# Decoding of the weights: the conversion from bfloat16 to float16 on GpSimd in place of ScalarE

## The chip, the core and the metric

The kernel runs on one core of a Trainium2 chip (trn2). The core has five engines, each with an instruction queue of its own: TensorE (PE, matmuls; PEld is its weight load), VectorE (DVE), ScalarE (ACT), GpSimd (POOL) and SyncE (SP, which here only issues DMAs). An engine works through its queue in order, and a semaphore holds an instruction back until what it needs has been done elsewhere. The metric is the device time of one execution in microseconds (us), lower is better.

## What is computed

Random-feature attention over 8 batches of 8 heads, and a feed-forward block on its output:

```python
def _attn_ref(q, k, v, omega):
    m, D = omega.shape
    scale = 1.0 / np.sqrt(np.sqrt(D))
    q_s, k_s = (q * scale, k * scale)
    def phi(x):
        proj = np.einsum('bhsd,md->bhsm', x, omega)
        sq = np.sum(x * x, axis=-1, keepdims=True) / 2.0
        h = proj - sq
        h = h - np.max(h, axis=-1, keepdims=True)
        return np.exp(h) / np.sqrt(m)
    q_p, k_p = (phi(q_s), phi(k_s))
    kv = np.einsum('bhsm,bhsd->bhmd', k_p, v)
    z = np.sum(k_p, axis=2)
    num = np.einsum('bhsm,bhmd->bhsd', q_p, kv)
    den = np.einsum('bhsm,bhm->bhs', q_p, z)[..., None] + 1e-06
    return num / den

def _moe_ref(x, w_in, w_out):      # x: 4608 x 512, d_ff 2048
    h = x @ w_in
    g = h - np.tanh(h)
    return g @ w_out
```

All inputs are float32. Batch 8, 8 heads, 576 positions, head size 64, 128 features.

## The kernel before

**Tiling.** The 4608 tokens go through in ten chunks (two of 256, eight of 512). The feed-forward block splits d_ff = 2048 into 16 slices of 128, called f0 to ff in the order strings. For each chunk and slice TensorE makes `h` (line 563, 12 matmuls, as each float32 product is made of three: high by high, high by low, low by high part), ScalarE takes the tanh, VectorE subtracts, ScalarE rounds the result to a high part, VectorE makes the low part, and TensorE then adds the slice to the output sums `po` (lines 589 to 591, 12 matmuls).

**The order.** Nothing is left to a scheduler. Two strings list every step: ORDER covers the first chunks, where batches 0 and 1 of the attention, the decoding of the weights and the first pass over the 16 slices are mixed; LATER covers the rest. A token `d4.b.0` reads: unit d (decoder) of slice 4, step b, argument 0. Each engine's queue holds its instructions in the order of the tokens, whatever the engine.

**The decoder.** The weights of all 16 slices come in once, at the start, and each slice is decoded in five steps before its first use:

- `is` (line 1130): two DMAs, issued by ScalarE, bring the slice's 128 x 2048 float32 words into `raw`, shifted by one 16-bit word.
- `b` (line 1134): the upper half of every second word, read as bfloat16 (1024 elements per partition, 8 bytes apart), is halved and written as float16 into every other 16-bit place of `head`. There are two heads, used in turn: even slices take head0, odd ones head1.
- `v` (line 1138, VectorE): `raw` shifted right by 13 bits, or-ed with `head`, gives `a` (1024 words). Both inputs lie in SBUF.
- `hi` (line 1143, ScalarE): 256 times `a`, rounded, is the high part of the weights `w`.
- `lo` (line 1146, VectorE): 256 times `a` less the high part; both inputs lie in SBUF.

The first pass over the slices has its g steps on lines 572 (`th`, ScalarE: tanh of `h`), 574 (`g`, VectorE: one input in PSUM, one in SBUF), 576 (`gh`, ScalarE) and 578 (`gl`, VectorE: both inputs in SBUF).

**GpSimd before.** Beside setting constants and clearing the heads (line 1174) at the start it copies small pads into `k_v` (line 962, 8 times) and scales 24 blocks of 128x128 query features (line 1078, step nA, which TensorE's transposes of line 1084 need). Its last such block stands ahead of slice f3 of the first pass; from there to the end it only clears six small tiles.

```python
        def bits(slot):
            u["a"] = dec.tile([P, 2 * DM], U32, tag=f"a{slot}", name=f"a{f}")
            nc.vector.scalar_tensor_tensor(out=u["a"], in0=u["raw"].bitcast(U32)[:, 0::2], scalar=13, in1=u["t"],
                                           op0=ALU.logical_shift_right, op1=ALU.bitwise_or)
```

The functions that the change touches follow.

Of the kernel before, what the change touches and what calls it, by code (L numbers as in the profile page):

```python
# [12 lines left out]
F16 = mybir.dt.float16  # L13
BF16 = mybir.dt.bfloat16
U32 = mybir.dt.uint32
AF = mybir.ActivationFunctionType
ALU = mybir.AluOpType
# [358 lines left out]
def favor_attention_ffn(ctx: ExitStack, tc: tile.TileContext, qT, kT, va, vt, omT, w, out):  # L376
# [12 lines left out]
    nc = tc.nc  # L389
# [8 lines left out]
    def open_pool(name, side="right"):  # L398
        pools[name] = tc.tile_pool(name=name, bufs=1, side=side, reuse_waits="tile")
        return pools[name].__enter__()  # L400

    def close_pool(name):
        pools.pop(name).__exit__(None, None, None)
# [108 lines left out]
    def weight_places(pool, fs):  # L512
        for f in fs:
            places[f] = pool
# [605 lines left out]
    def decoder(f):  # L1120
        u = {}

        def issue():
            if f >= NW and f not in places:
                close_pool("ka")
                weight_places(open_pool("w1", "left"), range(NW, NF))
            u["raw"] = places[f].tile([P, 8 * DM], U16, tag=f"w{f}", name=f"raw{f}")
            words = w[f].bitcast(U16)
            for j, n in enumerate((4 * DM, 4 * DM - 1)):
                nc.scalar.dma_start(u["raw"][:, 4 * DM * j : 4 * DM * j + n], words[:, 4 * DM * j + 1 : 4 * DM * j + n + 1])  # L1130

        def b(slot):
            u["t"] = heads[slot]
            nc.scalar.activation(u["t"].bitcast(F16)[:, 1::2], u["raw"].bitcast(BF16)[:, 2::4], AF.Copy, scale=0.5)

        def bits(slot):
            u["a"] = dec.tile([P, 2 * DM], U32, tag=f"a{slot}", name=f"a{f}")
            nc.vector.scalar_tensor_tensor(out=u["a"], in0=u["raw"].bitcast(U32)[:, 0::2], scalar=13, in1=u["t"],
                                           op0=ALU.logical_shift_right, op1=ALU.bitwise_or)

        def hi():
            wt[f] = places[f].tile([P, 2, 2 * DM], F32R, tag=f"w{f}", name=f"w{f}")
            nc.scalar.activation(wt[f][:, 0], u["a"].bitcast(F32), AF.Copy, scale=256.0)

        def lo():
            nc.vector.scalar_tensor_tensor(out=wt[f][:, 1], in0=u["a"].bitcast(F32), scalar=256.0,
                                           in1=wt[f][:, 0].bitcast(F32), op0=ALU.mult, op1=ALU.subtract)

        return {"is": issue, "b": b, "v": bits, "hi": hi, "lo": lo}
# [98 lines left out]
```

## Time and profile before

| what | before |
|---|---|
| median of 3 runs | 967.22 us (967.03 to 967.51) |
| the profiled execution, its own time | 967.64 us |
| its span, first to last instruction | 965.8 us |
| PE busy | 958.4 us (99%) |
| DVE busy | 740.2 us (77%) |
| ACT busy | 624.0 us (65%) |
| POOL busy | 17.3 us (2%) |
| line 1134, the moved step | 16 instructions, 14.6 to 109.4 us |

All numbers on rows come from the one profiled execution. Times in a view count from the start of its span. A busy share says how long an engine had an instruction in work, not whether anyone waited for it; matmuls are pipelined and their ends are modelled, so a PE that is busy all the time may still be held by a matmul that waits. "x2" behind a row means that two instructions in a row were merged, and "[0.81 <-DVE q_phi L1073]" that the engine stood idle for 0.81 us ahead of the row until VectorE's line 1073 released it.

### The profile page before, as it was taken

What the parts mean: (1) busy time and instruction counts of PE and PEld (TensorE: products, weight loads), DVE (VectorE), ACT (ScalarE), POOL (GpSimd) and SP (SyncE); (2) the same over time, 40 slices, a digit from 0 to 9 for tenths busy, and PEclk for the clock granted to TensorE, in tenths of its full rate; (3) what the DMA queues carried; (4) which work ended last, traced back from release to release, by engine and by line L of the source; (5) the groups of instructions that cost most, each with busy time, mean ns of one, the idle gap of its engine ahead of it and who ended that gap; (6) DMA issues with size and microseconds to landing.
All of it is one profiled execution on the core that took longest, in us unless ns stands there. A gap on an engine that the chain in (4) does not pass through costs nothing.

```text
span 965.8 us, 16378 instructions
## 1 busy us (share of the span) xinstructions
PE 958.4 (99%) x5024; PEld 793.0 (82%) x5024; DVE 740.2 (77%) x2773; ACT 624.0 (65%) x1626; POOL 17.3 (2%) x49
## 2 busy tenths in 40 slices
PE   9999999999999999999999999999999999999998
PEld 8778888888888888888888888888888887878886
DVE  5889799999998899788889989798976465443222
ACT  7988688887885778676676687676854354323222
POOL 2220000000000000000000000000000000000000
PEclk9999999999999999999999999999999999999999
DMA  8366444454544444543534436444543232221001
GB/s 294 117 214 233 166 103 148 128 136 125 135 127 139 108 114 130 153 117 96 151 88 115 120 91 168 118 110 121 144 103 93 56 110 66 55 55 44 0 1 44
DMA packets 94713, 112.00 MB, mean 116 GB/s; under 512 B 11169, under 2 KB 59681, under 8 KB 94625
## 3 DMA queue, kind: packets, MB, share of 16 engines
q1 hardware_dynamic: 89456, 93.49, 35.5%
q10 hardware_dynamic: 5168, 17.46, 5.2%
q8 instruction: 40, 0.66, 0.3%
q14 instruction: 49, 0.39, 0.2%
HBM read 79.31 MB, written 31.60 MB: 115 GB/s over the span
## 4 chain that ended last, share of the span: by engine, by line
PE 97%; DVE 1%; ACT 1%; issue 0%; DVEq 0%; ACTq 0%
PE h L563 41%; PE po L590 13%; PE po L589 13%; PE po L591 13%; PE pj_q L627 3%; PE pk L786 3%; PE pn L698 3%; PE pj_k_B L460 1%; PE pj_k_A L460 1%; PE k_pk L994 1%; PE k_pj L971 1%; PE q_pt L1084 1%; PE q_pn L1095 1%; PE q_pj L1046 0%; PE warm L426 0%; PE pj L590 0%
## 5 line engine op out<-in xcount | busy, mean ns | idle before, releaser
L563 PE MATMUL h<-xa,w 128*128 128x512 f32 (+1 forms) x1752 | 418.2, 388 | 0.0
L563 PEld LDWEIGHTS h<-xa,w 128*128 128x128 f32 x1752 | 321.8, 188 | 65.4 <-DVE zf L717 0.8
L589 PE MATMUL po<-w,zr 128*128 128x512 f32 x544 | 212.6, 391 | 0.0
L590 PE MATMUL po<-w,zr 128*128 128x512 f32 x544 | 212.6, 391 | 0.0
L591 PE MATMUL po<-w,zr 128*128 128x512 f32 x544 | 212.2, 390 | 0.0
L894 ACT ACTIVATE zf<-h 128x512 f32<-128x512 f32 x133 | 79.2, 595 | 195.2 <-PE h L563 190.6
L895 DVE TENSOR_TENSOR zf<-h,zf 128x512 f32<-128x512 f32 x133 | 91.6, 688 | 146.7 <-ACT zf L894 145.5
L591 PEld LDWEIGHTS po<-w,zr 128*128 128x128 f32 x544 | 102.1, 188 | 22.0
L589 PEld LDWEIGHTS po<-w,zr 128*128 128x128 f32 x544 | 102.2, 188 | 18.9
L590 PEld LDWEIGHTS po<-w,zr 128*128 128x128 f32 x544 | 102.2, 188 | 18.2
L896 ACT CAST zr<-zf 128x512 fp32r<-128x512 f32 x133 | 82.8, 622 | 45.3 <-DVE zf L895 43.9
L897 DVE TENSOR_TENSOR zr<-zf,zr 128x512 fp32r<-128x512 f32 x133 | 91.1, 685 | 26.1 <-ACT zr L896 25.0
L646 ACT ACTIVATE phi_q<-phi_q,nb_q 128x128 f32<-128x128 f32 x240 | 80.5, 394 | 27.2 <-DVE nb_q L639 26.5
L659 DVE CUSTOM_DVE_ANT_0 zf<-phi_q,zb 128x128 f32<-128x128 f32 (+1 forms) x240 | 59.4, 285 | 3.0 <-ACT phi_q L646 2.0
L639 DVE CUSTOM_DVE_ANT_1 phi_q<-pj_q,phi_q 128x128 f32<-128x128 f32 x240 | 56.9, 283 | 1.7 <-ACT phi_q L634 1.5
L634 ACT COPY phi_q<-pj_q 128x256 f32<-128x256 f32 x120 | 40.5, 376 | 11.2 <-PE pj_q L627 11.1
L627 PE MATMUL pj_q<-om,qx 128*128 128x256 f32 x240 | 41.2, 284 | 0.0
L627 PEld LDWEIGHTS pj_q<-om,qx 128*128 128x128 f32 x240 | 35.8, 188 | 4.7 <-issue 0.9
L667 DVE STREAM_TRANSPOSE phi_q<-phi_q 128x512 f32<-128x512 f32 x60 | 38.1, 666 | 0.0
L477 ACT ACTIVATE phi_kA<-phi_kA,nb_k_A 128x128 f32<-128x128 f32 x96 | 33.0, 395 | 6.0 <-DVE nb_k_A L471 5.9
L477 ACT ACTIVATE phi_kB<-phi_kB,nb_k_B 128x128 f32<-128x128 f32 x96 | 31.5, 395 | 1.8 <-DVE nb_k_B L471 1.7
L698 PE MATMUL pn<-phi_q,kvw 128*64 128x64 f32 (+4 forms) x272 | 26.8, 341 | 0.0
(156 smaller groups left out, 1250.4 us busy)
## 6 DMA issues: line engine op xcount, KB each, us to landing
turned<-phi_q SPq DMA_DIRECT2D x120, 128.0 KB
phi_q<-turned SPq DMA_DIRECT2D x60, 256.0 KB
raw<-w ACTq DMA_DIRECT2D x16, 512.0 KB
raw<-w ACTq DMA_DIRECT2D x16, 511.8 KB
qf<-qT SPq DMA_DIRECT2D x30, 256.0 KB
v<-vt SPq DMA_DIRECT2D x24, 320.0 KB
kf<-kT SPq DMA_DIRECT2D x24, 288.0 KB
turned_k<-cz SPq DMA_DIRECT2D x96, 64.0 KB
```

Source lines behind the costliest of these rows:

```text
L477: nc.scalar.activation(u[kind][:, at + i], u[kind][:, at + i], AF.Exp, bias=w["nb"][:, i : i + 1], scale=-1.0)
L563: nc.tensor.matmul(o, w_, x, start=i == 0, stop=i == len(prods) - 1)
L589: nc.tensor.matmul(po[t], gh[:, 2 * j + t % 2 if both(ch, s) else t], wt[f][:, 0, DM:], start=first, stop=False)
L590: nc.tensor.matmul(po[t], gh[:, 2 * j + t % 2 if both(ch, s) else t], wt[f][:, 1, DM:], start=False, stop=False)
L591: nc.tensor.matmul(po[t], gl[:, 2 * j + t % 2 if both(ch, s) else t], wt[f][:, 0, DM:], start=False, stop=last)
L627: nc.tensor.matmul(u["pj", t][:, h], u["x"][:, h, t * P : (t + 1) * P], om2, start=True, stop=True)
L646: nc.scalar.activation(ph, ph, AF.Exp, bias=u["nb", t][:, h : h + 1], scale=-1.0)
L659: nc.vector.tensor_tensor_reduce(quarters(junks[h][r]), u["ph"][r, h, :, t], quarters(kvs[b, k][1][r, h]), scale=1.0, scalar=EPS, op0=ALU. ...
L894: th=lambda: nc.scalar.activation(g, blocks(u["p"])[:, 0:n], AF.Tanh),
L895: g=lambda: nc.vector.tensor_sub(g, blocks(u["p"])[:, 0:n], g),
L896: gh=lambda: nc.scalar.copy(gh, g),
L897: gl=lambda: nc.vector.tensor_sub(gl, g, gh.bitcast(F32)))
```

## The change

Step `b` of the decoder is written for GpSimd in place of ScalarE, for all 16 slices. The tokens of ORDER stay as they are, so the step keeps its place among them. Input, output and result are the same; the second multiplication is by 1.

```diff
         def b(slot):
             u["t"] = heads[slot]
-            nc.scalar.activation(u["t"].bitcast(F16)[:, 1::2], u["raw"].bitcast(BF16)[:, 2::4], AF.Copy, scale=0.5)
+            nc.gpsimd.tensor_scalar(u["t"].bitcast(F16)[:, 1::2], u["raw"].bitcast(BF16)[:, 2::4], 0.5, 1.0, op0=ALU.mult, op1=ALU.mult)
```

The queues of TensorE, VectorE and SyncE hold the same instructions in the same order as before. On ScalarE 16 instructions are gone. On GpSimd, the first place is among the scalings of the query blocks of the last native query units (q21 and q20; `head` is the float16 tile, `raw` the fetched words, `q_phi` the features, `q_dn` their denominators):

```order
 L1078 TENSOR_SCALAR q_phi_693<-q_phi_693,q_dn_752 128x128
+L1134 TENSOR_SCALAR head_111<-raw_438 128x1024
 L1078 TENSOR_SCALAR q_phi_880<-q_phi_880,q_dn_891 128x128
 L1078 TENSOR_SCALAR q_phi_873<-q_phi_873,q_dn_891 128x128
+L1134 TENSOR_SCALAR head_112<-raw_850 128x1024
 L1078 TENSOR_SCALAR q_phi_931<-q_phi_931,q_dn_953 128x128
 L1078 TENSOR_SCALAR q_phi_918<-q_phi_918,q_dn_953 128x128
```

The steps of slices 2 (`raw_438`) and 3 (`raw_850`) now stand between scalings, which were next to one another.

The second place on GpSimd is behind the last scalings, where the first pass over the slices is on:

```order
 L1078 TENSOR_SCALAR q_phi_931<-q_phi_931,q_dn_1038 128x128
 L1078 TENSOR_SCALAR q_phi_918<-q_phi_918,q_dn_1038 128x128
+L1134 TENSOR_SCALAR head_111<-raw_963 128x1024
+L1134 TENSOR_SCALAR head_112<-raw_1003 128x1024
+L1134 TENSOR_SCALAR head_111<-raw_1020 128x1024
+L1134 TENSOR_SCALAR head_112<-raw_1062 128x1024
+L1134 TENSOR_SCALAR head_111<-raw_1124 128x1024
```

The steps of slices 4 to 8 are shown; those of 9 to 15 follow them in the same way, and nothing stands between them.

On ScalarE, the same stretch (the `w` rows are step hi, the `zf` and `zr` rows tanh and rounding of a slice's g):

```order
 L576 CAST zr<-zf 128x512
-L1134 ACTIVATE head_111<-raw_963 128x1024
 L1130 DMA raw_1062<-w 128x2048
 L1130 DMA raw_1062<-w 128x2047
 L1106 COPY zf<-q_pn 128x512
-L1134 ACTIVATE head_112<-raw_1003 128x1024
 L1143 ACTIVATE w_1085<-a_1081 128x1024
 L572 ACTIVATE zf<-h_3_1066 128x512
 L1143 ACTIVATE w_1103<-a_1087 128x1024
-L1134 ACTIVATE head_111<-raw_1020 128x1024
 L576 CAST zr<-zf 128x512
-L1134 ACTIVATE head_112<-raw_1062 128x1024
```

The rows of slices 4 to 7 are taken out, and what stood behind each moves up; the DMAs of `raw` stay on ScalarE.

## Rows read from the trace of the kernel before

**Rows 1.** The page: busy time and share of the span of each engine, and the chain of work that ended last, by engine.
```profile
PE 958.4 (99%) x5024; PEld 793.0 (82%) x5024; DVE 740.2 (77%) x2773; ACT 624.0 (65%) x1626; POOL 17.3 (2%) x49
...
PE 97%; DVE 1%; ACT 1%; issue 0%; DVEq 0%; ACTq 0%
```
**Rows 2.** Who waited for whom from 0 to 130 us: waiting engine and line, the one waited for, us in total, times, longest.
```profile
DVE a L1138 <- ACT head L1134: 3.9, 6, 0.8
...
PE k_pk L1021 <- ACT k_kvw L1013: 1.3, 1, 1.3
...
PE q_pt L1084 <- DVE q_phi L1073: 0.8, 1, 0.8
...
ACT k_kvw L1013 <- DVE k_z L1009: 0.8, 1, 0.8
```
**Rows 3.** Busy time of each engine by stage: start and end, length, then PE, PEld, DVE, ACT and POOL busy with their counts, granted PE clock, DMA share, GB/s.
```profile
0.00:60.00 60.00, 57.32 (x526) 48.66 (x527) 45.02 (x162) 51.26 (x163) 12.73 (x37) 1.00 0.56 183
60.00:72.00 12.00, 11.19 (x64) 8.56 (x63) 11.52 (x53) 9.15 (x13) 3.96 (x6) 1.00 0.88 325
...
72.00:117.00 45.00, 45.00 (x214) 36.81 (x213) 38.45 (x41) 36.06 (x44) 0.57 (x7) 1.00 0.62 212
```
**Rows 4.** The instructions of line 1134 in the whole span: count, shortest, median and longest in ns, first and last start.
```profile
L1134 ACT ACTIVATE head<-raw x16: 1356/1377/1567, 14.6 to 109.4; 128x1024 f16<-128x1024 bf16 x16
```
**Rows 5.** VectorE from 72 to 117 us, by line: busy us and mean ns, then idle us just before them and who ended it.
```profile
L1138 DVE SCALAR_TENSOR_TENSOR a<-raw,head 128x1024 uint32<-128x1024 uint32 x12 | 14.6, 1230 | 3.5 <-ACT head L1134 3.3
L1146 DVE SCALAR_TENSOR_TENSOR w<-a,w 128x1024 fp32r<-128x1024 f32 x12 | 14.4, 1221 | 2.0 <-ACT w L1143 2.0
L578 DVE TENSOR_TENSOR zr<-zf,zr 128x512 fp32r<-128x512 f32 x8 | 5.5, 686 | 0.9 <-ACT zr L576 0.9
L574 DVE TENSOR_TENSOR zf<-h,zf 128x512 f32<-128x512 f32 x8 | 5.5, 684 | 0.1
```
**Rows 6.** GpSimd's instructions by line, whole span: count, busy us, mean ns.
```profile
L1078 POOL TENSOR_SCALAR q_phi<-q_phi,q_dn 128x128 f32<-128x128 f32 x24 | 12.4, 529 | 36.5 <-DVE q_dn L1068 19.6 <-DVE q_dn L1065 8.9 <-ACT head L1134 3.3
L1174 POOL MEMSET head<- 128x1024 uint32 x2 | 1.8, 953 | 0.0
L962 POOL COPY k_v<-pads 128x20 f32<-128x20 f32 x8 | 1.7, 214 | 18.2 <-DMA k_v<-va 18.2
```
**Rows 7.** GpSimd's instructions in order of time: start, length, line, operation. The two rows at 30 us are the first, and the second alone, of a pair that runs back to back.
```profile
0.87 1.84 POOL L1174 MEMSET head<- 128x1024 uint32 x2
...
27.05 0.98 POOL L1078 TENSOR_SCALAR q_phi<-q_phi,q_dn 128x128 f32<-128x128 f32 x2 [1.92 <-DVE q_dn L1068]
...
30.42 0.37 POOL L1078 TENSOR_SCALAR q_phi<-q_phi,q_dn 128x128 f32<-128x128 f32 x1 [1.38 <-ACT k_zb L1026]
30.77 0.41 POOL L1078 TENSOR_SCALAR q_phi<-q_phi,q_dn 128x128 f32<-128x128 f32 x1
...
57.20 1.76 POOL L1078 TENSOR_SCALAR q_phi<-q_phi,q_dn 128x128 f32<-128x128 f32 x2 [11.80 <-DVE q_dn L1068]
...
70.01 1.70 POOL L1078 TENSOR_SCALAR q_phi<-q_phi,q_dn 128x128 f32<-128x128 f32 x1 [4.11 <-DVE q_dn L1068]
...
70.01 2.13 POOL L1078 TENSOR_SCALAR q_phi<-q_phi,q_dn 128x128 f32<-128x128 f32 x2 [4.11 <-DVE q_dn L1068]
```
**Rows 8.** VectorE in order of time, beside the GpSimd rows of 27 and of 70 us, with the run from 59 us and the last slice of the first pass.
```profile
26.45 0.28 DVE L1065 CUSTOM_DVE_ANT_0 junk<-q_phi,k_zb 128x128 f32<-128x128 f32 x1
26.66 0.07 DVE L1065 DVE_READ_ACCUMULATOR2_ANT q_dn<- 128x1 f32 x1
...
27.06 0.31 DVE L1065 CUSTOM_DVE_ANT_0 junk<-q_phi,k_zb 128x128 f32<-128x128 f32 x1
27.30 0.08 DVE L1065 DVE_READ_ACCUMULATOR2_ANT q_dn<- 128x1 f32 x1
27.30 0.36 DVE L1065 CUSTOM_DVE_ANT_0 zf<-q_phi,k_zb 128x128 f32<-128x128 f32 x1
27.59 0.08 DVE L1065 DVE_READ_ACCUMULATOR2_ANT q_dn<- 128x1 f32 x1
...
59.06 0.69 DVE L578 TENSOR_TENSOR zr<-zf,zr 128x512 fp32r<-128x512 f32 x1 [0.26 <-ACT zr L576]
...
69.76 1.20 DVE L1146 SCALAR_TENSOR_TENSOR w<-a,w 128x1024 fp32r<-128x1024 f32 x1
70.87 0.68 DVE L578 TENSOR_TENSOR zr<-zf,zr 128x512 fp32r<-128x512 f32 x1
71.47 0.51 DVE L1073 TENSOR_SCALAR q_phi<-q_phi,q_dn 128x128 f32<-128x128 f32 x2
71.90 1.31 DVE L1138 SCALAR_TENSOR_TENSOR a<-raw,head 128x1024 uint32<-128x1024 uint32 x1
...
116.20 0.69 DVE L578 TENSOR_TENSOR zr<-zf,zr 128x512 fp32r<-128x512 f32 x1 [0.69 <-ACT zr L576]
```
**Rows 9.** The chain of work that ended last, near 119 us: start, length, engine and line. The first matmul of the sums of slice fa.
```profile
116.15 2.72 PE h L563 x12
118.87 0.23 PE po L589
```

## The prediction

> **What bounds the kernel now.** The page comes first: TensorE is busy 99% of the span and the chain that ended last is 97% TensorE [rows 1]. So an engine that is relieved gives time back only where TensorE stood waiting for it, and an engine that is loaded costs time as soon as TensorE starts to wait for it. The list of waits, read next for its PE rows, shows how little there is to win: up to 130 us, TensorE waited 1.3 us for ScalarE's line 1013 and 0.8 us for VectorE's line 1073, and line 1013 had itself waited 0.8 us for VectorE [rows 2]. The busy time by stage, read third, shows where there is something to lose: from 72 to 117 us, while the first pass over the slices runs and the decoder works ahead of it, TensorE is busy all 45.0 us, VectorE 38.45, ScalarE 36.06 and GpSimd 0.57 [rows 3]. VectorE is the second engine to watch, and 12 of the 16 moved steps (slices 4 to 15) lie in that stage or at its edge.
>
> **What is taken away.** 16 instructions of 1.38 us leave ScalarE, 22 us in all [rows 4]. Where the wait for it ended last, this shows as VectorE's line 1138 waiting for head, 3.9 us in six waits [rows 2], of them 3.3 after 72 us [rows 5]; that time VectorE gets back if the step is ready earlier, and it is counted below as idle time of that stage. For TensorE I take nothing: of the 1.3 us that it waited for line 1013, 0.8 stood on VectorE behind it, so at most 0.5 us is ScalarE's [rows 2].
>
> **What is added: the length of one step on GpSimd.** No row shows a conversion of 1024 elements there. From below: a memset of 128x1024, which reads nothing, 0.92 us (1.84 for two) [rows 7]. From above: two scalings of 128x128, the same operation as the new one, start 0.35 us apart [rows 7], and eight times that is 2.8 us. Between them: a copy of 20 elements takes 0.214 us [rows 6], a scaling of 128 takes 0.37 [rows 7]; the difference, 0.156 us for 108 elements, is 1.44 ns for each, and 0.21 + 1004 x 1.44 ns gives 1.7 us. I take this one, because it splits the fixed part from the part that grows, in the same operation. The Trainium skill (GPSIMD Engine Reference, Engine selection) says that operations with one input run there at about the line rate; at its clock of 1.2 GHz that would be an estimate of 0.85 us for a step, and the sum below would come out at no loss. The trace speaks against it: at that rate 128 elements would be 0.11 us, and scalings follow one another at 0.35 [rows 7].
>
> **Where it lies: beside VectorE, not under it.** The rows at 70 us decide. A scaling of 128x128 that takes 0.37 us alone took 1.70 us: it started at 70.01 under VectorE's line 1146 and ended at 71.71, just after that and line 578 behind it had run out at 71.55 [rows 7, 8]. Both read two operands from SBUF. Earlier, at 57.2 us, two scalings took 1.76 us instead of 0.76 [rows 7]. So GpSimd makes no headway while VectorE streams two SBUF operands. In the other direction the rows show less: while two scalings ran at 27.05 us, the starts of VectorE's line 1065 came 0.24 and 0.29 us apart instead of 0.21, a loss of 0.11 us, 0.055 for each scaling [rows 7, 8]. The Trainium skill (SBUF — State Buffer, Who interferes with whom) has it stricter: whichever of the two starts first keeps the shared read port for its whole instruction. By that each step would hold VectorE up for all of its length; by the rows at 27 us, scaled by eight, for 0.44 us; the first gives my forecast, the second the first rival. I take full exclusion, since the step has to end before line 1138 of its slice can start and cannot run under 1138, 1146 or 578 of the slices before: whoever yields, the times add.
>
> **The sum for 72 to 117 us.** VectorE's lines with two SBUF operands take 14.6 + 14.4 + 5.5 = 34.5 us [rows 5]. Its groups with line 574 add to 40.0 and the stage shows 38.45 [rows 3], so some 1.5 us is overlap of neighbours, and 33.0 us remain. Twelve steps of 1.7 us are 20.4. Together 53.4 us in a stage of 45.0: **+8.4**. Line 574 (5.5 us, one operand in PSUM) and the idle gaps can lie beside the steps and are counted so already. VectorE's 2.0 us of waiting for ScalarE's step hi [rows 5] remain, since hi still follows 1138 and lo follows hi, and the chance that a step fits just there is poor: **+2.0**. At the stage's end TensorE has room: the last line 578 ends at 116.89, and the sums of slice fa start at 118.87 [rows 8, 9]: **-2.0**. At the start, the step of slice 4 stands in GpSimd's queue behind the last two scalings, which end at 72.14 [rows 7], while line 1138 of that slice began at 71.90 [rows 8]: **+0.2**.
>
> **The four steps before.** Slice 0's step fits between GpSimd's copies, where VectorE reads PSUM; slices 1 and 2 likewise run ahead of their old places. I cost these at nothing: GpSimd's 12.73 us of work in 60 cover little [rows 3], and what would be lost if that cover were gone is one length each, 1.7 us. Slice 3 is the exception. Its step follows the scalings that end at 58.96 and meets line 578 at 59.06 and the short two-operand instructions behind it [rows 7, 8]. VectorE's lateness there goes to TensorE at once, for its 0.8 us wait near 65 us is for VectorE's line 1073 [rows 2]. I take one length, 1.7, less the 0.6 us of waits for head that vanish before 72 us: **+1.1**. Behind this step in GpSimd's queue stand the next query scalings, for which TensorE's transposes wait; the lateness is the same one and isn't counted twice.
>
> Sum: 8.4 + 2.0 - 2.0 + 0.2 + 1.1 = 9.7 us. The profiled execution took 967.64 us, so 977.3; the median of the runs is 0.42 lower, so 977. Behind 117 us TensorE is busy without a gap, so nothing of this is made up later.
>
> **The rivals.**
>
> *VectorE hardly yields (no change).* If a step on GpSimd lets VectorE's second operand through and costs it only the 0.44 us scaled from 27 us, 12 steps add 5.3 us, and 33.0 + 5.3 = 38.3 stays below 45. TensorE then sees nothing, and the time is 967, at best 966.7 with ScalarE's 0.5 us. It decides in the stage from 72 us at (45.0 - 33.0) / 12 = 1.0 us of the port for a step: below that the work fits. For it: the small losses at 27 us. Against it: the 1.70 us row.
>
> *The step is short.* Between the memset's 0.92 us and 1.3: at 0.92 the stage holds 33.0 + 11.0 = 44.0, the first term is gone, the next two cancel, and 0.2 + 0.3 remain: 967.7; at 1.2, 33.0 + 14.4 is 2.4 over, and with 0.2 + 0.6 it is 970.4. For it: elements of 16 bits instead of 32. Against it: a stride of 8 bytes in and 4 out.
>
> *The step is long.* At 2.8 us 33.6 us are added: 21.6 over, and 2.2 + 0.2 more, 991. For it: the 0.35 us between scalings, if all of that grows with the size.
>
> *ScalarE's relief pays.* If the waits of TensorE up to 130 us, 1.3 and 0.8, went entirely, the time would be 965.1. Against it: both lead back to VectorE.
>
> **How the numbers follow.** Forecast (full exclusion, step of 1.3 to 2.1 us, 972 to 982): 0.56. VectorE hardly yields: 0.14. Short step: 0.15. Long step: 0.11. Relief pays: 0.04. Each tenth of a microsecond in the length moves the time by 1.3 us. The range reaches from 967.0, which takes in the short step and half of the first rival, to 986, a step of 2.4 us. A difference of 0.2% (1.9 us) is about what a measurement of this kernel can tell from none, so "same" is 965.3 to 969.1: the first rival and some 0.09 of the short step, 0.23; faster 0.04; slower 0.73.
>
> **What the profile after would show.** GpSimd's line 1134 at about 1.7 us where VectorE leaves it alone, and longer beneath lines 1138, 1146 and 578; VectorE's two-operand lines lengthened, or waiting for head, or both; TensorE with gaps from about 73 us on, ended by line 578 or 576 of the slices, and its first pass over the slices ending some 9 to 10 us later. ScalarE's hi would follow line 1138 without delay. I am wrong if TensorE has no gaps between 72 and 120 us, if line 1134 takes under 1 us, or if the time is lost in another stage, as in the scalings ahead of the transposes.

## The result and the profile after

The changed kernel takes 974.28 us (median of 6 runs, 973.55 to 975.02) against 967.37 us before (967.03 to 968.0): a ratio of 1.0072, 95% interval 1.0062 to 1.0083, or 6.9 us slower. The profiled execution took 973.55 us with a span of 971.8, 6.0 us above that of before. The page, in the lines that answer to [rows 1]:

```profile
PE 959.9 (99%) x5024; PEld 792.5 (82%) x5024; DVE 748.5 (77%) x2773; ACT 605.2 (62%) x1610; POOL 44.8 (5%) x65
...
PE 90%; DVE 7%; DMA 1%; issue 1%; ACT 1%; POOL 0%; DVEq 0%; POOLq 0%; ACTq 0%
```

ScalarE is 19 us lighter and GpSimd 27.5 us heavier, but the number to look at is VectorE's: 8.3 us more busy time in the same 2773 instructions, and 7% of the chain that ended last instead of 1%. The waits of TensorE up to 130 us, which answer to [rows 2], say at which places it came to matter:

```profile
PE q_pt L1084 <- DVE q_phi L1073: 2.2, 2, 1.1
PE po L591 <- DVE zr L578: 1.8, 3, 0.9
PE k_pk L1021 <- ACT k_kvw L1013: 1.3, 1, 1.3
PE h L563 <- ACT w L1143: 1.1, 1, 1.1
```

The wait for line 1013 stands as before. New are a wait of 1.1 us for line 1073 at 46.7 us, beside the one of before, which has grown from 0.8 to 1.1, the waits for line 578, and one for hi (line 1143). The step itself, by the rows of its line (count, shortest, median, longest in ns, first and last start):

```profile
L1134 POOL TENSOR_SCALAR head<-raw x16: 1334/1650/2397, 11.9 to 116.0; 128x1024 f16<-128x1024 bf16 x16
```

It takes 1.33 to 1.38 us where nobody is in its way, which is as long as on ScalarE [rows 4], and up to 2.4 us where VectorE is. VectorE by line from 72 to 124 us (the same stage, now longer; 13 and 9 instructions of lines 1146 and 578 fall into it), which answers to [rows 5]:

```profile
L1146 DVE SCALAR_TENSOR_TENSOR w<-a,w 128x1024 fp32r<-128x1024 f32 x13 | 18.2, 1419 | 1.0 <-ACT w L1143 1.0
L1138 DVE SCALAR_TENSOR_TENSOR a<-raw,head 128x1024 uint32<-128x1024 uint32 x12 | 18.0, 1514 | 4.1 <-POOL head L1134 3.5 <-POOL columns L1198 0.7
L578 DVE TENSOR_TENSOR zr<-zf,zr 128x512 fp32r<-128x512 f32 x9 | 7.2, 805 | 0.7 <-ACT zr L576 0.7
L574 DVE TENSOR_TENSOR zf<-h,zf 128x512 f32<-128x512 f32 x8 | 5.4, 679 | 0.0
```

The three lines with two SBUF operands have grown (1.42 from 1.22 us on average, 1.51 from 1.23, 0.81 from 0.69); line 574, with one operand in PSUM, has not. At the old means the 34 instructions would be 13 x 1.221 + 12 x 1.230 + 9 x 0.686 = 36.8 us, at the new ones they are 43.9, so VectorE spends some 7 us inside its own instructions held up. Its waits for head, on the other hand, are about what they were.

One stretch shows both directions. GpSimd, in order of time (steps of slices 4 and 5 as a pair, of which the second started at 74.55 us, then 6 and 7):

```profile
73.23 2.68 POOL L1134 TENSOR_SCALAR head<-raw 128x1024 f16<-128x1024 bf16 x2
77.00 4.53 POOL L1134 TENSOR_SCALAR head<-raw 128x1024 f16<-128x1024 bf16 x2 [1.10 <-DVE a L1138]
```

and VectorE beside it:

```profile
74.64 3.41 DVE L1138 SCALAR_TENSOR_TENSOR a<-raw,head 128x1024 uint32<-128x1024 uint32 x2 [1.54 <-POOL head L1134]
78.04 2.26 DVE L1146 SCALAR_TENSOR_TENSOR w<-a,w 128x1024 fp32r<-128x1024 f32 x1
80.22 0.68 DVE L574 TENSOR_TENSOR zf<-h,zf 128x512 f32<-128x512 f32 x1
80.82 1.73 DVE L1146 SCALAR_TENSOR_TENSOR w<-a,w 128x1024 fp32r<-128x1024 f32 x1
```

VectorE waits 1.54 us for slice 4's step, starts line 1138 under slice 5's, and the pair of 1138 takes 3.41 us instead of the 2.35 to 2.44 that it takes undisturbed. Line 1146 at 78.04 takes 2.26 instead of 1.22, and GpSimd's steps 6 and 7 need 2.3 us each. Each of the two stands still while the other reads. Which of them gets in first differs: by these lengths GpSimd's step 6 went ahead of line 1146 although that line stood right behind line 1138, while in the kernel before a scaling at 70 us had waited through two such lines in a row [rows 7, 8].

**Where along the program the time goes.** The start of the first `h` matmul (line 563) of slice f0, of f3 and of the slice that the order strings write f0b, read from TensorE in order of time, in us. f0b is slice b of the same chunk, the twelfth of the first pass: ORDER ends with slice fa, and LATER begins with b. (The text put on record for e6 calls it the next chunk's first slice, which is wrong; the times are not touched by that.) A whole trace can lie some 0.5 us off before f0 (the kernel with slices 4 to 15 alone on GpSimd does the same as before up to there and began f0 at 52.22, but f3 at 70.08), so f0 to f3 is uncertain by as much:

| kernel | f0 | f3 | f0b | f0 to f3 | f3 to f0b |
|---|---|---|---|---|---|
| before | 51.75 | 70.06 | 115.99 | 18.31 | 45.93 |
| after | 52.61 | 71.18 | 122.08 | 18.57 | 50.90 |
| e1, no step | 51.00 | 68.52 | 114.45 | 17.52 | 45.93 |
| e2, extra step, read | 52.79 | 71.96 | 123.70 | 19.17 | 51.74 |
| e3, extra write | 52.58 | 71.07 | 117.60 | 18.49 | 46.53 |
| e4, half steps | 52.28 | 70.25 | 117.24 | 17.97 | 46.99 |
| e5, slices 0 to 3 | 52.28 | 70.85 | 116.77 | 18.57 | 45.92 |
| e6, slices 4 to 15 | 52.22 | 70.08 | 121.84 | 17.86 | 51.76 |
| e7, one operation | 52.31 | 73.28 | 129.33 | 20.97 | 56.05 |
| e8, double steps | 52.20 | 71.82 | 136.95 | 19.62 | 65.13 |
| e10, slices 0 to 2, early | 51.12 | 68.68 | 114.63 | 17.56 | 45.95 |
| e11, slices 0 to 3, early | 51.92 | 69.66 | 116.16 | 17.74 | 46.50 |
| e13, all, 2 and 3 early | 51.86 | 69.58 | 121.38 | 17.72 | 51.80 |

So 1.1 us of the change's loss is there at f3, and 5.0 us come up between f3 and f0b.

### The profile page after: what moved, and what is told of

It reads as the page before. It is cut to its first block, busy times and chain, and to the rows that moved or that the text cites. A ratio compares the mean times of both kernels' runs of the same rounds, so it can differ in the third digit from the quotient of the medians.

```text
span 971.8 us, 16394 instructions
## 1 busy us (share of the span) xinstructions
PE 959.9 (99%) x5024; PEld 792.5 (82%) x5024; DVE 748.5 (77%) x2773; ACT 605.2 (62%) x1610; POOL 44.8 (5%) x65
## 4 chain that ended last, share of the span: by engine, by line
PE 90%; DVE 7%; DMA 1%; issue 1%; ACT 1%; POOL 0%; DVEq 0%; POOLq 0%; ACTq 0%
PE h L563 38%; PE po L590 12%; PE po L591 12%; PE po L589 12%; PE pj_q L627 3%; PE pk L786 3%; PE pn L698 3%; DMA raw<-w 1%; DVE a L1138 1%; DVE w L1146 1%; PE pj_k_B L460 1%; PE pj_k_A L460 1%; PE k_pk L994 1%; DVE zr L578 1%; DVE junk L1065 0%
## 5 line engine op out<-in xcount | busy, mean ns | idle before, releaser
L1134 POOL TENSOR_SCALAR head<-raw 128x1024 f16<-128x1024 bf16 x16 | 27.9, 1748 | 22.2 <-DMA raw<-w 21.0
```

## The experiments

All ratios are to the kernel before on the same chip, with their 95% intervals. A wait on `raw` that an extra reader brings falls on step hi, which overwrites `raw`.

**e1: the step left out.**

```diff
-            nc.scalar.activation(u["t"].bitcast(F16)[:, 1::2], u["raw"].bitcast(BF16)[:, 2::4], AF.Copy, scale=0.5)
```

> The step of line 1134 is left out on both engines, so the heads stay at zero and the weights that are used are wrong in their upper bits; everything else runs. It shows what ScalarE's relief alone is worth. Theory (the loss comes from GpSimd's and VectorE's use of SBUF, the relief is worth nothing): 966.7 to 967.4 us against 967.4 before, TensorE's idle time as before within 1 us. Rival (ScalarE was holding TensorE up, and the change would gain but for the new load): 964 to 966 us.

965.9 us, ratio 0.9985 (0.9976 to 0.9994). That is below the theory's range and inside the rival's, near its upper end: the relief by itself is worth 1.45 us, more than I had allowed it. It lies ahead of f3 alone; from f3 to f0b nothing is won. TensorE's wait for line 1073 (0.8 us) is gone. VectorE had been late there, as I read the rows, because line 1138 had waited for ScalarE in the kernel before, 0.58 us at 53 us; no run separates that:

```profile
53.74 1.23 DVE L1138 SCALAR_TENSOR_TENSOR a<-raw,head 128x1024 uint32<-128x1024 uint32 x1 [0.58 <-ACT head L1134]
```

The rest of the gain is there at f0; TensorE's wait for line 1013 is 0.5 us shorter (0.8 instead of 1.3).

**e2: the step on ScalarE, and once more on GpSimd for nobody.**

```diff
             nc.scalar.activation(u["t"].bitcast(F16)[:, 1::2], u["raw"].bitcast(BF16)[:, 2::4], AF.Copy, scale=0.5)
+            nc.gpsimd.tensor_scalar(spare.bitcast(F16)[:, 1::2], u["raw"].bitcast(BF16)[:, 2::4], 0.5, 1.0, op0=ALU.mult, op1=ALU.mult)
```

> The step stays on ScalarE as before; GpSimd does the same conversion once more, from raw into a spare tile that nobody reads. Line 1138 does not wait for GpSimd. Theory (VectorE's lines with two SBUF operands and GpSimd's reading instruction exclude one another): 972 to 975 us, lines 1138, 1146 and 578 again reach 1.7 to 2.4 us where they fall under a GpSimd step. Rival (the loss is the wait for the step, queued on GpSimd behind its scalings and late DMAs): 967 to 968.5 us, the VectorE rows at 1.2 us.

975.42 us, ratio 1.0082 (1.0068 to 1.0096). The loss is all there, and a little more, though line 1138 waits for nobody on GpSimd. VectorE by line from 72 to 124 us:

```profile
L1147 DVE SCALAR_TENSOR_TENSOR w<-a,w 128x1024 fp32r<-128x1024 f32 x13 | 21.0, 1632 | 1.4 <-ACT w L1144 1.3
L1139 DVE SCALAR_TENSOR_TENSOR a<-raw,head 128x1024 uint32<-128x1024 uint32 x12 | 16.2, 1364 | 2.3 <-ACT head L1134 2.3
L578 DVE TENSOR_TENSOR zr<-zf,zr 128x512 fp32r<-128x512 f32 x8 | 7.7, 957 | 0.0
```

(Lines 1147 and 1139 are 1146 and 1138 of before.) The growth has moved from the line that waits for the step to whichever two-operand line comes along. Step hi does wait for the extra read, 3.1 us in two places, but VectorE does not wait longer for hi because of it (1.3 us, 2.0 before [rows 5]), and in e3 hi waits for GpSimd too and little is lost. So the rival, a wait behind another queue, falls as the cause of the loss. The little more has a part that is not VectorE's: from 84.5 to 87.6 us, behind TensorE's waits of 0.6 and 1.4 us, the granted clock of TensorE lies at 1.2 instead of 2.4 GHz, and its matmuls start 0.43 us apart instead of 0.23, about 1.5 us by these rows. In the changed kernel the clock stays at 2.4 GHz.

**e3: GpSimd writes as much, and reads one element.**

```diff
             nc.scalar.activation(u["t"].bitcast(F16)[:, 1::2], u["raw"].bitcast(BF16)[:, 2::4], AF.Copy, scale=0.5)
+            nc.gpsimd.tensor_copy(spare[:, 0:1], u["raw"].bitcast(U32)[:, 0:1])
+            nc.gpsimd.memset(spare.bitcast(F16)[:, 1::2], 0)
```

> The step stays on ScalarE; GpSimd copies one element of raw to a spare tile, which paces it, and then clears 1024 places of the spare tile, every other half word, so it writes as the step does but reads next to nothing. Nobody reads the tile. Theory (what is contended is the reading of SBUF): 967 to 968.5 us, VectorE's two-operand rows at 1.2 and 0.7 us. Rival (any long GpSimd instruction that touches SBUF holds VectorE up): 970 to 975 us.

969.66 us, ratio 1.0024 (1.0015 to 1.0034): beyond the theory's range and short of the rival's. The rows divide it. VectorE by line from 72 to 124 us, then two rows from VectorE in order of time, and GpSimd beside the second:

```profile
L1140 DVE SCALAR_TENSOR_TENSOR a<-raw,head 128x1024 uint32<-128x1024 uint32 x12 | 14.6, 1230 | 3.1 <-ACT head L1134 2.8
L1148 DVE SCALAR_TENSOR_TENSOR w<-a,w 128x1024 fp32r<-128x1024 f32 x12 | 14.4, 1222 | 2.7 <-ACT w L1145 2.7
```
```profile
44.21 0.45 DVE L1073 TENSOR_SCALAR q_phi<-q_phi,q_dn 128x128 f32<-128x128 f32 x2
...
45.18 1.54 DVE L1073 TENSOR_SCALAR q_phi<-q_phi,q_dn 128x128 f32<-128x128 f32 x2
```
```profile
45.36 1.28 POOL L1136 MEMSET spare<- 128x1024 f16 x1
```

The two-operand lines are as before: writing alone does not hold them. But line 1073, a scaling with one tensor operand, takes 1.54 us for a pair instead of 0.45 under a GpSimd instruction that reads nothing. So there are two kinds of meeting, and the second accounts, by the rows, for most of the 1.0 us by which f3 is late. The 0.6 us behind f3 stands beside the longer wait of line 1148 for hi (2.7 us against 2.0 [rows 5]), which waits here for the little copy (2.4 us in three places); I did not separate that. The copy itself shows the other direction at its plainest. One element takes 0.19 us where VectorE is not in the way, and 1.17 us under the pair of line 1140 that VectorE ran from 72.94 us:

```profile
34.50 0.19 POOL L1135 COPY spare<-raw 128x1 uint32<-128x1 uint32 x1
...
73.12 1.17 POOL L1135 COPY spare<-raw 128x1 uint32<-128x1 uint32 x1
```

The Trainium skill (SBUF — State Buffer, Who interferes with whom) has both: two SBUF inputs contend only with a GpSimd instruction that reads, and a scaling on VectorE can run in a mode that takes the shared ports whatever GpSimd does with them. The trace agrees, with 1.22 us and 1.54 us.

**e4: half of each step on each engine.**

```diff
-            nc.gpsimd.tensor_scalar(u["t"].bitcast(F16)[:, 1::2], u["raw"].bitcast(BF16)[:, 2::4], 0.5, 1.0, op0=ALU.mult, op1=ALU.mult)
+            nc.gpsimd.tensor_scalar(u["t"].bitcast(F16)[:, 1:1024:2], u["raw"].bitcast(BF16)[:, 2:2048:4], 0.5, 1.0, op0=ALU.mult, op1=ALU.mult)
+            nc.scalar.activation(u["t"].bitcast(F16)[:, 1025::2], u["raw"].bitcast(BF16)[:, 2050::4], AF.Copy, scale=0.5)
```

> Each step is cut in two: GpSimd converts the first 512 elements, ScalarE the last 512, all slices. Theory (the time goes where twelve steps and VectorE's 33 us of two-operand work together pass 45 us, that is at 1.0 us for each step): GpSimd's half takes about 0.75 us, twelve are 9 us, 42 us fit into 45, so most of the 5 us lost from 72 us on is back; 968 to 970.5 us, the rest from slices 2 and 3, whose halves still meet VectorE. Rival (each meeting costs what it costs, loss in proportion to the length): 970.5 to 971.5 us. Rival (the loss is the wait behind another queue): 973 to 975 us, as with the whole step.

968.8 us, ratio 1.0015 (1.0006 to 1.0024), in the theory's range. GpSimd's half takes 0.77 us at the shortest:

```profile
L1134 POOL TENSOR_SCALAR head<-raw x16: 765/800/1733, 11.5 to 110.2; 128x512 f16<-128x512 bf16 x16
```

From f3 to f0b the loss is 1.1 us instead of 5.0: a length of 57% leaves 21% of the loss.

**e8: each step twice.**

```diff
             nc.gpsimd.tensor_scalar(u["t"].bitcast(F16)[:, 1::2], u["raw"].bitcast(BF16)[:, 2::4], 0.5, 1.0, op0=ALU.mult, op1=ALU.mult)
+            nc.gpsimd.tensor_scalar(u["t"].bitcast(F16)[:, 1::2], u["raw"].bitcast(BF16)[:, 2::4], 0.5, 1.0, op0=ALU.mult, op1=ALU.mult)
```

> Each step is done twice on GpSimd, the second time over the first. Theory (the sum of the prediction: 33 us of VectorE's two-operand work and twelve times 2.7 us of GpSimd's do not fit into 45, and each us in a step's length costs 12): 33 + 32.4 - 45 = 20 us over, with the small terms 987 to 993 us. Rival (each step costs in proportion to its length, with no threshold): twice the loss of the change, 980 to 983 us. Rival (only the wait for the step counts): 978 us at most, and VectorE's lines not longer than with the single step.

989.5 us, ratio 1.0222 (1.0208 to 1.0236). From f3 to f0b it loses 19.2 us, where the sum has 20.4, and 3.9 times the loss of single steps. VectorE by line from 70 to 140 us:

```profile
L1147 DVE SCALAR_TENSOR_TENSOR w<-a,w 128x1024 fp32r<-128x1024 f32 x13 | 23.1, 1794 | 1.1 <-ACT w L1144 1.1
L1139 DVE SCALAR_TENSOR_TENSOR a<-raw,head 128x1024 uint32<-128x1024 uint32 x12 | 20.6, 1725 | 6.8 <-POOL head L1135 6.1 <-POOL columns L1199 0.6
L578 DVE TENSOR_TENSOR zr<-zf,zr 128x512 fp32r<-128x512 f32 x9 | 9.4, 1046 | 0.7 <-ACT zr L576 0.7
```

Not all of the 19.2 us is exclusion. Behind TensorE's longer waits its granted clock falls from 2.4 to 1.2 GHz in three stretches (80 to 84, 104 to 108 and 132 to 138 us), which it does neither in the changed kernel nor with half steps. Start and end, length, TensorE's busy time with its count, granted clock (1.00 is 2.4 GHz), DMA share, GB/s:

```profile
126.00:130.00 4.00, 3.06 (x14) 1.00 0.00 0
130.00:134.00 4.00, 2.22 (x6) 0.71 0.00 0
134.00:138.00 4.00, 4.00 (x11) 0.50 0.00 0
```

In the last of them the matmuls ahead of f0b start 0.43 us apart instead of 0.23, which puts some 2 us on f0b; the 1.4 us of the stretch at 104 us may be hidden in part. By these rows I estimate that 2 to 3.5 of the 19.2 us are the clock's, and that the sum, with 20.4, is some 3 to 5 us too high for the exclusion alone.

Half, single and double lengths (about 0.77, 1.35 and 2.7 us) lose 1.1, 5.0 and 19.2 us: up to the half length 1.4 us for each us of length, over the next piece 6.7, and over the last 10.5, or 8 to 9 without the clock. That is a stage that fills up and then runs over, not a price for each meeting.

**e5 and e6: the step on GpSimd for slices 0 to 3, or for 4 to 15, alone.**

```diff
+            if f < 4:                # e6: f >= 4
+                nc.gpsimd.tensor_scalar(u["t"].bitcast(F16)[:, 1::2], u["raw"].bitcast(BF16)[:, 2::4], 0.5, 1.0, op0=ALU.mult, op1=ALU.mult)
+            else:
+                nc.scalar.activation(u["t"].bitcast(F16)[:, 1::2], u["raw"].bitcast(BF16)[:, 2::4], AF.Copy, scale=0.5)
```

> Slices 0 to 3 take the step on GpSimd, at the places of the change; slices 4 to 15 on ScalarE as before. In the changed kernel the matmuls of slice f3 began 1.1 us late. Theory (two separate losses: slices 2 and 3 meet VectorE before 72 us, the other twelve overfill the stage from 72 us on): 968.2 to 968.9 us, and f3 late by 1.1 us again, later slices by no more. Rival (the later stage suffers from what was lost before it): 969 to 971 us.

> Slices 4 to 15 take the step on GpSimd, slices 0 to 3 on ScalarE as before. Theory: the stage from 72 us on loses its 5 us alone, 972 to 973.5 us; f3 not late, f0b (the next chunk's first slice) late by 5 us. Rival (the loss comes from the four early steps and is only carried on): under 970 us.

e5: 968.73 us, ratio 1.0014 (1.0005 to 1.0023). e6: 973.27 us, ratio 1.0057 (1.0044 to 1.0070). Against 967.45 us that is 1.3 and 5.8 us, together 7.1 for the change's 6.9: two losses in two places, whose medians add. The table, with one execution of each, has the places (e5 loses nothing behind f3, e6 nothing ahead of it), but not so clean a sum: behind f3 e6 loses 5.8 us and the change 5.0, in an execution that was the fastest of its six.

**e10, e11, e13: the early steps moved up.** ORDER is edited: slice 2's step stands right behind slice 1's; in e11 and e13 slice 3's stands ahead of the query scalings of 57 us as well. e10 has slices 0 to 2 on GpSimd, e11 0 to 3, e13 all. The lines are those of e11 and e13; in e10 `d3.b.1` stays where it was.

```diff
-q00.redA q20.lq.0 q00.redB d1.b.1 k11.pk1 d0.lo q11.xh q10.pt0.3 k11.kvwa k11.kvf k12.pj.4.5.7 q11.xl q00.expA.1 k11.z
+q00.redA q20.lq.0 q00.redB d1.b.1 d2.b.0 k11.pk1 d0.lo q11.xh q10.pt0.3 k11.kvwa k11.kvf k12.pj.4.5.7 q11.xl q00.expA.1 k11.z
...
-f0.h.4 q21.redB d2.b.0 q21.redA q21.expB.2 d2.v.0 q21.expA.3 k13.pk1 f0.th q21.den0 d2.hi f1.h.5 k13.kvwa k13.kvf f0.g
+f0.h.4 q21.redB q21.redA q21.expB.2 d2.v.0 q21.expA.3 k13.pk1 f0.th q21.den0 d3.b.1 d2.hi f1.h.5 k13.kvwa k13.kvf f0.g
```

> Slices 0, 1 and 2 take the step on GpSimd, and slice 2's is moved up to stand right behind slice 1's, at 35 us, where VectorE reads PSUM; slices 3 to 15 on ScalarE as before. Without the step altogether the kernel won 1.4 us, half of it before f0. Theory (a step on GpSimd is free where VectorE has neither two SBUF operands nor line 1073 on hand, and then ScalarE's relief shows): 966.3 to 967.2 us, line 1073 not above 0.5 us for a pair. Rival (ScalarE's relief by three steps is worth nothing): 967.3 to 967.6 us.

> As with slices 0 to 2 early, and slice 3 on GpSimd too, moved ahead of the query scalings of 57 us, to where its data land (56 us); slices 4 to 15 on ScalarE. Theory (what matters is whom a step meets): beside it VectorE runs short two-operand instructions of line 1065 with gaps between them, so a step costs part of its length there; against that ScalarE is relieved once more: 966.2 to 967.0 us, no better than with three slices by more than 0.3. Rival (each step taken from ScalarE wins): 965.9 us, as without the step.

> The changed kernel, all slices on GpSimd, with the steps of slices 2 and 3 moved up as in the kernel with four early slices. Theory (the two losses add): the early loss turns into the gain of the early relief, the loss from 72 us on stays: 972 to 973 us. Rival (the stage from 72 us on is bound by VectorE and makes the early gain good for nothing): 973.5 to 974.5 us.

e10: 966.65 us, ratio 0.9991 (0.9982 to 1.0000). The steps of slices 1 and 2 run from 34.06 to 36.72 us beside nothing that they meet, and line 1073 is free again. GpSimd and VectorE in order of time:

```profile
34.06 2.66 POOL L1135 TENSOR_SCALAR head<-raw 128x1024 f16<-128x1024 bf16 x2
```
```profile
44.79 0.47 DVE L1073 TENSOR_SCALAR q_phi<-q_phi,q_dn 128x128 f32<-128x128 f32 x2
```

Of the versions that do the whole step it is the fastest, 0.8 us below the kernel before, at the edge of what its interval allows. e11: 967.12 us, ratio 0.9995 (0.9986 to 1.0004), just beyond the theory's range and no better than e10; slice 3's step meets the end of line 1065 and line 1146 (1.49 us at 56.96 us) and gives the relief back. It also lost 0.6 us between f9 and f0b, where it differs from e10 in nothing but its past; I did not find out why. e13: 972.4 us, ratio 1.0050 (1.0037 to 1.0063), in the theory's range: the early loss is gone, and f3 to f0b loses 5.9 us as in e6.

**e12: the last DMAs issued sooner.** `de.is` and `df.is` are moved to stand behind `dd.is`, in the changed kernel.

```diff
-f6.gh db.b.1 f7.h.0 f6.gl q20.xh.6 db.v.1 da.hi db.hi da.lo f6.o f7.th db.lo dd.is dc.b.0 f7.g f8.h.6 f7.gh dc.v.0
-de.is f7.gl dc.hi f7.o df.is dc.lo f8.th dd.b.1 f8.g f8.gh f9.h.7 dd.v.1 f8.gl dd.hi de.b.0 dd.lo f8.o f9.th de.v.0
+f6.gh db.b.1 f7.h.0 f6.gl q20.xh.6 db.v.1 da.hi db.hi da.lo f6.o f7.th db.lo dd.is de.is df.is dc.b.0 f7.g f8.h.6 f7.gh dc.v.0
+f7.gl dc.hi f7.o dc.lo f8.th dd.b.1 f8.g f8.gh f9.h.7 dd.v.1 f8.gl dd.hi de.b.0 dd.lo f8.o f9.th de.v.0
```

> The changed kernel, with the DMA issues of slices 14 and 15 moved up on ScalarE's queue, right behind slice 13's. In the changed kernel the last 1.0 us of the loss came up at 119.7 us, where TensorE waited for line 578 behind line 1138 of slice 15, whose step had waited for its DMA. Theory (the DMAs, issued from a queue that the loss itself has made late, add that last 1 us): 973.0 to 973.6 us. Rival (VectorE is full there anyway): 974 to 974.6 us, as without the edit.

973.76 us, ratio 1.0066 (1.0054 to 1.0079), between the two ranges, and it cannot be told from the change's 1.0072. TensorE's waits for line 578 fall from 1.8 to 1.1 us, the one near 119.7 us being gone, but f3 to f0b still takes 50.8 us (50.9 in the change), and slice 15's step still waited for its DMA (1.48 us). Whether the DMAs add to the loss at the end stays open.

**e7: one multiplication in the step instead of two.**

```diff
-            nc.gpsimd.tensor_scalar(u["t"].bitcast(F16)[:, 1::2], u["raw"].bitcast(BF16)[:, 2::4], 0.5, 1.0, op0=ALU.mult, op1=ALU.mult)
+            nc.gpsimd.tensor_scalar(u["t"].bitcast(F16)[:, 1::2], u["raw"].bitcast(BF16)[:, 2::4], 0.5, None, op0=ALU.mult)
```

> The changed kernel with a single multiplication in the step, the second one (by 1) dropped. If the length of a step goes with the number of operations, it falls below 1.35 us and the time by about 12 us for each us: at 1.1 us some 971 us. If it goes with the elements that are read and written, the length stays at 1.35 us and the time at 974.3 us. I expect the second.

979.35 us, ratio 1.0123 (1.0109 to 1.0137). Both readings were wrong: with less to do the step takes more than twice as long. Its rows, then VectorE beside the steps of slices 4 to 6, of which the second starts at 76.79 us:

```profile
L1134 POOL TENSOR_SCALAR head<-raw x16: 3114/3155/4216, 11.8 to 120.3; 128x1024 f16<-128x1024 bf16 x16
```
```profile
76.88 2.07 DVE L1138 SCALAR_TENSOR_TENSOR a<-raw,head 128x1024 uint32<-128x1024 uint32 x1 [3.29 <-POOL head L1134]
79.94 2.07 DVE L1138 SCALAR_TENSOR_TENSOR a<-raw,head 128x1024 uint32<-128x1024 uint32 x1 [0.98 <-POOL head L1134]
81.94 1.21 DVE L1146 SCALAR_TENSOR_TENSOR w<-a,w 128x1024 fp32r<-128x1024 f32 x1
```

Line 1138, started 0.09 us behind a step of 3.1 us, ends after 2.07 us: it was held for 0.85 us, and then ran while the step was still going. And line 1146 ran its 1.21 us under the third of these steps, all but its end. So a step does not hold VectorE for its whole length. That goes with the loss from f3 to f0b: 10.1 us at 3.1 us a step, less than at the 2.7 us of the double steps. It is not one cause, though. VectorE waits 6.1 us for the longer step (3.5 in the change), and TensorE's granted clock lies at 1.2 GHz from 67.5 to 71 and from 125.4 to 129 us, which by the starts of its matmuls costs about 1.5 us each time, the second within the 10.1.

## Why the prediction was right

The forecast was 977 us in a range of 967 to 986, and slower with a chance of 0.73; it came to 974.28. The loss measured is 6.9 us, the sum had 9.7. The range reached from no change to a step of 2.4 us, so that the time lies in it says little by itself; what counts is the mechanism and the terms.

- **The mechanism** held: VectorE's two-operand lines and GpSimd's reads exclude one another. e2 shows it where line 1138 does not wait for GpSimd, e3 shows the same lines untouched when GpSimd only writes, and e8 and e4 show the filling up of the stage. In the changed kernel's rows the exclusion is plain in the direction that was thin before: 1.1 us on lines 1138, 1146 and 578 at the most (2.31, 2.33 and 1.79 us the longest).
- **The term that was mis-sized is the length of a step:** 1.7 us by a split between a copy of 20 elements and a scaling of 128; it is 1.35. With 1.35, 33.0 + 16.2 is 4.2 over instead of 8.4, and slice 3's term is 0.75 instead of 1.1; the sum is 5.2 and the profiled execution 972.8, against 973.55 measured. The rate of 1.44 ns for an element was too high. The fixed part carried over: 512 elements take 0.77 us (e4) and 1024 take 1.35, which is 1.13 ns for each element and 0.19 us besides, close to the 0.21 that was taken from the copy.
- **The small terms of the stage** (the start behind the scalings, lo's wait for hi, the room at the end) came to about what they should in sum: 5.0 us from f3 to f0b, for 4.2 + 0.2. One by one they were not: VectorE waited 1.0 us for hi instead of 2.0, and 3.5 us for the step, a wait that the sum had taken as gained back. That they came out in sum is luck.
- **"Slices 1 and 2 cost nothing" failed for slice 2.** Its step ran at 45.16 us, and line 1073 took 1.51 us for a pair where it had taken 0.47; TensorE then waited 1.1 us for it. I had counted only instructions with two SBUF operands as exposed. The early 1.1 us that I had put on slice 3 came out right in size by luck, of other parts: slice 2's meeting, slice 3's meeting with line 578 (1.71 us at 59.16 us), and the relief against them. VectorE and GpSimd around slice 2's step:

```profile
45.20 1.51 DVE L1073 TENSOR_SCALAR q_phi<-q_phi,q_dn 128x128 f32<-128x128 f32 x2
```
```profile
45.16 1.33 POOL L1134 TENSOR_SCALAR head<-raw 128x1024 f16<-128x1024 bf16 x1
...
59.03 1.36 POOL L1134 TENSOR_SCALAR head<-raw 128x1024 f16<-128x1024 bf16 x1
```

- **"For TensorE I take nothing" from ScalarE's relief was too low:** e1 puts it at 1.45 us, about the size of the change's early loss. For 0.8 us of it the chain runs, as I read the rows, from ScalarE's step over line 1138 and VectorE's queue to line 1073 and TensorE, one link further back than I followed it.
- **The rivals.** "VectorE hardly yields" falls to e2. "The step is short" was right by half: 1.35 us is just past its end. "The step is long" falls. "Relief pays" is true by itself (e1, e10) and outweighed. That a step holds VectorE up for all of its length, from which the forecast came, holds loosely: a step of 1.35 us holds it for up to 1.1, one of 3.1 us for 0.85.

## What to carry to other kernels

An idle engine is not a free engine: before work goes to GpSimd, list what VectorE does at that moment, and count as exposed both its instructions with two SBUF operands and its one-operand scalings from SBUF to SBUF. Add the times in which the two engines exclude one another over the stage. While the sum stays well below the stage the move costs little (1.1 us at half the length); past it the loss grows fast, here by 7 to 9 us for each microsecond in the length of twelve steps. If the work must move, place it by what VectorE is doing and not by where the token stood: three steps beside PSUM work came out 0.8 us faster, where sixteen lost 6.9. And read the granted clock beside each run: in e2, e7 and e8 it fell behind TensorE's waits, and part of their loss was the clock's.

## What the runs showed of the hardware

- GpSimd converts 1024 elements from bfloat16 to float16 with two multiplications (0.5 and 1.0) in 1.33 to 1.38 us, 512 in 0.77, and with one multiplication in 3.11 to 3.18 us where it is alone. What makes the shorter form slower, no run here shows.
- Under a GpSimd memset of 1.28 us VectorE's lines with two SBUF operands kept their 1.22 us, and its scaling of 128x128 was held for about 1.1 us.
- A GpSimd copy of one element takes 0.19 us alone and 1.17 us where VectorE runs an instruction with two SBUF operands beside it.
- How long GpSimd holds VectorE's second operand is not the length of its instruction: up to 1.1 us of 1.35 in the one form, 0.85 of 3.1 in the other.
- TensorE's granted clock fell to 1.2 GHz for 3 to 7 us at a time behind longer waits in e2, e7 and e8; its 512-column matmuls then start 0.43 us apart instead of 0.23. In the changed kernel it stayed at 2.4 GHz.
